# Linear attention y: the three transposes of the diagonal term ahead of the half-array matmuls

## The chip, the cores and the metric

One core of one Trainium2 chip runs the whole program. The metric is the device time of one execution in microseconds (us), taken as the median of several executions. The profile comes from one execution more, with the hardware profiler on.

## The reference, cut to what matters

Three layers follow each other: a linear attention with decay (4 batches, 8 heads, 768 steps, head size 48), a mixture of experts with causal softmax attention, and a channel mix. The change touches the first layer alone:

```python
for t in range(S):
    cur = u * k[t] (outer) v[t]              # the diagonal term
    y[t] = r[t] @ (state + cur)
    state = w[t][:, None] * state + k[t] (outer) v[t]
```

The kernel cuts the 768 steps into 6 chunks of 128. Within a chunk, y is the sum of three terms: the diagonal term (a number per step and head times v), the products of the chunk's earlier steps (`at`, a masked 128x128 matrix, times v), and, from the second chunk on, the state that came in (`um`) times r.

## The kernel before, in words

**Stages.** Stage A is the linear attention, one pair of heads at a time, 16 pairs in all. Stage B is the mixture of experts, one batch at a time. Stage C is the channel mix. Batch 0 of A runs by itself with the loading of B's weights; then the rest of A (`sA`) is woven with B (`sB`) and with the conversion of C's weights to two parts (`conv`). Once A is through, `c_weights` (L819 to L826) loads C's weights with DMAs from GpSimd, and the rest of B is woven with C.

**What sets the order.** `run_all` (L88) takes the next piece from the stream that is least far by written costs; `weave` (L75) puts the preparation of the next pair (`a_prep`) between the pieces of the present one (`a_pair`). That gives the order in which the program is written down. The framework then places each instruction on its engine's queue by its own estimate of when it can start, so an engine's queue holds nearly, but not exactly, the written order; an instruction that is ready early can come ahead of one that waits. Each engine then works its queue off in order.

**A pair of heads.** `a_prep` (L209) transposes w, k and r on TensorE (`ptr`, L201), runs two scans on VectorE (L220 `suf`, L246 `ex`) and makes the diagonal term `dg` on GpSimd (L261). `a_pair` (L318) calls `g_unit` three times (matmuls `pg` L329, copy on ScalarE L337, mask on GpSimd L338, result `at`), `a_u` once (matmuls `pu` L298, then `um` on VectorE L307 and L313) and `y_unit` twice, three chunks each; `a_kt` (transposes `pkt`, L286) belongs to the next pair.

**y_unit (L343 to L374).** One PSUM tile `py` holds three chunks of 128 columns side by side, head 0 in partitions 0 to 47 and head 1 in partitions 64 to 111. For each chunk in turn the diagonal term is transposed into its columns over the whole width of the array (L348, `dg` and the identity, 128x128); then matmuls add to it, each on one half of the array's columns (48 columns used, head 0 on the left half, head 1 on the right, L359): one of v and `at` per head, and, but for chunk 0, one of `um` and `rt` per head. The profile shows each of these fp32 matmuls as two instructions, so a chunk has one transpose and eight half-array instructions (four for chunk 0). Then ScalarE (L373) and VectorE (L374) split `py` into two parts `xs`, which go to HBM or into B's tile.

Other users of one half of the array's columns are `pu` (L298) and `pa` in B (L701). All other matmuls and transposes use its whole width.

Of the kernel before, what the change touches and what calls it, by code (L numbers as in the profile page):

```python
# [23 lines left out]
C = 128  # L24
# [88 lines left out]
def rwkv_moe_kernel(ctx, tc, r, k, v, w, u, wg, wq, wk, wv, wo, mu_k, mu_r, w_k, w_v, w_r, out):  # L113
    nc = tc.nc
# [20 lines left out]
    def ps_a(nm):  # L135
        tag = cyc["tags"][cyc["n"] % len(cyc["tags"])]
        cyc["n"] += 1
        return (psA if tag == "a" else ps).tile([128, 512], F32, tag=tag, name=nm, bufs=PSB[tag])
# [12 lines left out]
    ident = const.tile([128, 128], F32, name="ident")  # L151
# [126 lines left out]
    def a_kt(b, pr):  # L278
        kt = kts.pop((b, pr))
        n1 = NC_ - 1  # L280
        kh = pA.tile([128, n1 * 128], F32, tag="kh", name="kh", bufs=1)
        for c0, c1 in ((0, 3), (3, n1)):
            q = ps_a("pkt")
            m = (c1 - c0) * 128
            for c in range(c0, c1):
                nc.tensor.transpose(q[:, (c - c0) * 128 : (c - c0 + 1) * 128], kt[:, c * C : (c + 1) * C], ident)  # L286
            nc.scalar.copy(kh[:, c0 * 128 : c0 * 128 + m], q[:, 0:m])
        heads[b, pr] = kh

    def a_u(b, pr):  # L290
        rt, kt, vn, pc = prep[b, pr]
        kh = heads.pop((b, pr))
        n1 = NC_ - 1
        pu = ps_a("pu")
        for c in range(n1):
            for h in range(2):
                p0 = 64 * h
                nc.tensor.matmul(  # L298
                    pu[p0 : p0 + 64, c * D : (c + 1) * D],
                    lhsT=kh[:, c * 128 + p0 : c * 128 + p0 + 64],  # L300
                    rhs=vn[:, h * NC_ + c, 0:D],
                    start=True,
                    stop=True,
                )
        um = pA.tile([128, D * n1], F32, tag="um", name="um", bufs=2)
        uv = um.rearrange("p (d c) -> p d c", c=n1)
        nc.vector.tensor_tensor(  # L307
            out=uv,
            in0=pu[:, 0 : n1 * D].rearrange("p (c d) -> p d c", d=D),
            in1=pc[:, None, 1:NC_].to_broadcast([128, D, n1]),  # L310
            op=OP.mult,
        )
        nc.vector.tensor_tensor_scan(  # L313
            out=um, data0=pcxs[(b * NP + pr) % 2].rearrange("p d c -> p (d c)"), data1=um, initial=0.0, op0=OP.mult, op1=OP.add
        )
        return um

    def a_pair(b, pr, nxt):  # L318
        rt, kt, vn, pc = prep[b, pr]
        gs = []  # L320
        dg = dgs.pop((b, pr))
        xs = pA.tile([128, 2, S], F32R, tag="xs", name="xs", bufs=XSB)

        def g_unit(i):
            at = pA.tile([128, 2, 2, C], F32, tag="at", name="at", bufs=ATB)
            pg = ps_a("pg")
            for x in range(2):
                c = 2 * i + x
                nc.tensor.matmul(  # L329
                    pg[:, x * 2 * C : (x + 1) * 2 * C],  # L330
                    lhsT=kt[:, c * C : (c + 1) * C],
                    rhs=rt[:, c].rearrange("p h x -> p (h x)"),
                    start=True,
                    stop=True,
                )
            av = at.rearrange("p c h t -> p (c h t)")
            nc.scalar.copy(av, pg)  # L337
            nc.gpsimd.affine_select(  # L338
                out=av, in_=av, pattern=[[0, 4], [1, C]], compare_op=OP.is_gt, fill=0.0, base=0, channel_multiplier=-1
            )  # L340
            gs.append(at)

        def y_unit(i, um):  # L343
            py = ps_a("py")
            for x in range(3):
                c = 3 * i + x
                cols = slice(x * C, (x + 1) * C)
                nc.tensor.transpose(py[:, cols], dg[:, c].rearrange("p h x -> p (h x)"), ident)  # L348
                terms = []
                for h in range(2):  # L350
                    q = [(vn[:, h * NC_ + c], gs[c // 2][:, c % 2, h])]
                    if c > 0:
                        q.append((um[:, c - 1 :: NC_ - 1], rt[:, c, h]))
                    terms.append(q)
                n = len(terms[0])
                for j in range(n):
                    for h in range(2):
                        lt, rh = terms[h][j]
                        nc.tensor.matmul(  # L359
                            py[64 * h : 64 * h + D, cols],  # L360
                            lhsT=lt,
                            rhs=rh,
                            start=False,
                            stop=j == n - 1,
                            skip_group_check=True,
                        )
            sl = slice(i * HALF, (i + 1) * HALF)
            src, lo = py[:, 0:HALF], nc.vector
            if b * NP + pr in X_POOL:
                lo = nc.gpsimd  # L370
                src = xs[:, 1, sl].bitcast(F32)
                nc.scalar.copy(src, py[:, 0:HALF])
            nc.scalar.copy(xs[:, 0, sl], src)  # L373
            lo.tensor_tensor(out=xs[:, 1, sl], in0=src, in1=xs[:, 0, sl].bitcast(F32), op=OP.subtract)  # L374

        g_unit(0)
        yield 4 * 218
        um = a_u(b, pr)
        yield 10 * 110
        g_unit(1)  # L380
        yield 4 * 218
        g_unit(2)
        yield 4 * 218
        y_unit(0, um)
        yield 16 * 128
        if nxt is not None:
            a_kt(*nxt)
        yield 5 * 109
        y_unit(1, um)
        yield 18 * 128  # L390
        prep.pop((b, pr))
        for h in range(2):
            if b:
                f0 = (2 * pr + h) * D
                nc.sync.dma_start(
                    xd[b, :, f0 : f0 + D].rearrange("x p s -> p x s"), xs[64 * h : 64 * h + D].bitcast(F32)
                )
            else:
                o = 0
                while o < D:  # L400
                    kt_, p0 = divmod((2 * pr + h) * D + o, 128)
                    m = min(D - o, 128 - p0)
                    nc.sync.dma_start(
                        xts[0][p0 : p0 + m, :, kt_].bitcast(F32), xs[64 * h + o : 64 * h + o + m].bitcast(F32)
                    )
                    o += m
# [809 lines left out]
```

## Time and profile before

| | |
|---|---|
| median of 3 runs | 754.82 us (754.77 to 755.72) |
| the profiled execution: its own time | 753.42 us |
| the profiled execution: its span | 751.6 us |
| TensorE matmul busy | 692.0 us (92%) |
| VectorE busy | 502.2 us (67%) |
| ScalarE busy | 406.7 us (54%) |
| GpSimd busy | 293.5 us (39%) |
| TensorE's share of the chain that ended last | 66% |
| VectorE's share of that chain | 18% |

PE is TensorE's matmul, PEld its weight load, DVE VectorE, ACT ScalarE, POOL GpSimd, SP SyncE. The span is the time from the first to the last recorded instruction; the execution's own time is 1.8 us longer. The chain that ended last is followed back from the last instruction: at each step to what released it, or to the instruction ahead of it on its engine. Busy time of TensorE has modelled ends, so the distance from one start to the next is the better measure of what one of its instructions takes.

### The profile page before, as it was taken

Reading aid. Unit: us, or ns where it says so; the run is one execution under the profiler, and the core shown is the slowest. Engines: PE = TensorE matmul, PEld = TensorE weight load, DVE = VectorE, ACT = ScalarE, POOL = GpSimd, SP = SyncE. Lnnn points to the kernel's source line nnn. Section 1 sums busy time; section 2 is a strip of 40 time slices with the busy share of each in tenths; the row PEclk is TensorE's granted clock in tenths of the full one; section 3 lists DMA queues with packets and bytes.
Section 4 is the critical chain, followed back from the end, with each engine's and each line's share of the span. In section 5 each row is a group of like instructions: output and inputs, shape, how many; then the busy total and the mean of one; then the engine's idle time right before and its main releaser. Section 6 shows DMA issues by size and latency. Waiting matters only on the chain.

```text
span 751.6 us, 13686 instructions
## 1 busy us (share of the span) xinstructions
PE 692.0 (92%) x4938; PEld 590.2 (79%) x4938; DVE 502.2 (67%) x938; ACT 406.7 (54%) x1117; POOL 293.5 (39%) x397
## 2 busy tenths in 40 slices
PE   6998977989799999973999999999999999999996
PEld 4676755666577686752898998988999888999995
DVE  8989898898899759642474456756636674729620
ACT  3554564666566446642756466466554657453530
POOL 5966444233344222220635345344242525252320
PEclk8999988999899999995999999999999999999999
DMA  7788666669567552179021201060211020111001
GB/s 154 161 166 192 182 162 169 152 173 274 141 175 191 121 126 66 32 250 347 22 74 22 75 12 32 11 179 12 69 48 44 1 64 1 53 64 53 12 22 37
DMA packets 144205, 77.88 MB, mean 104 GB/s; under 512 B 109824, under 2 KB 138752, under 8 KB 143616
## 3 DMA queue, kind: packets, MB, share of 16 engines
q1 hardware_dynamic: 139936, 64.73, 33.9%
q0 software_dynamic: 864, 7.47, 2.5%
q10 hardware_dynamic: 3328, 4.72, 1.9%
q8 instruction: 41, 0.67, 0.4%
q14 instruction: 36, 0.29, 0.1%
HBM read 47.40 MB, written 23.99 MB: 95 GB/s over the span
## 4 chain that ended last, share of the span: by engine, by line
PE 66%; DVE 18%; DMA 6%; issue 3%; POOL 2%; ACT 2%; SPq 1%; DVEq 0%; POOLq 0%; ACTq 0%
PE ph L862 14%; PE pvo L862 13%; PE pa L701 6%; PE pz L862 5%; PE pq L509 4%; PE pt L672 4%; DVE suf L220 3%; PE py L359 3%; DMA k<-k 3%; PE po L509 3%; PE psc L615 3%; PE pv L509 2%; PE pg L329 2%; PE psc L616 2%; DVE ex L246 2%
## 5 line engine op out<-in xcount | busy, mean ns | idle before, releaser
L624 DVE TENSOR_REDUCE st<-psc 128x1 f32<-128x384 f32 (+4 forms) x128 | 62.5, 500 | 69.1 <-PE psc L620 61.0
L882 POOL TENSOR_TENSOR rl<-rl 128x256 f32<-128x256 f32 (+1 forms) x88 | 61.5, 702 | 100.1 <-ACT rl L881 96.6
L856 POOL TENSOR_TENSOR ml<-m,mh 128x256 fp32r<-128x256 f32 x54 | 40.6, 751 | 114.6 <-ACT mh L855 114.5
L636 ACT ACTIVATE A<-psc,st 128x384 f32<-128x384 f32 (+4 forms) x128 | 68.9, 543 | 27.1 <-DVE st L633 16.4
L862 PE MATMUL ph<-mh,ckh 128*128 128x256 f32 (+1 forms) x264 | 79.6, 302 | 2.1 <-DMA ckh<-ck_h_scratch 2.1
L862 PE MATMUL ph<-mh,ckl 128*128 128x256 f32 (+1 forms) x264 | 77.3, 293 | 0.0
L862 PE MATMUL ph<-ml,ckh 128*128 128x256 f32 (+1 forms) x264 | 77.2, 294 | 0.0
L338 POOL TENSOR_SCALAR_AFFINE_SELECT at<-at 128x512 f32<-128x512 f32 x48 | 41.7, 873 | 79.7 <-ACT at L337 79.3
L615 PE MATMUL psc<-k,q 128*128 128x384 f32 (+4 forms) x128 | 49.9, 390 | 20.9 <-DMA k<-k 15.7
L862 PE MATMUL pvo<-cvh,hh 128*128 128x384 f32 x192 | 65.1, 339 | 0.0
L862 PE MATMUL pvo<-cvl,hh 128*128 128x384 f32 x192 | 64.7, 337 | 0.0
L862 PE MATMUL pvo<-cvh,hl 128*128 128x384 f32 x192 | 64.3, 337 | 0.0
L885 POOL TENSOR_TENSOR hl<-rl,hh 128x256 fp32r<-128x256 f32 x72 | 53.3, 747 | 25.7 <-ACT hh L883 25.5
L329 PE MATMUL pg<-rt,kt 128*128 128x256 f32 x192 | 54.5, 412 | 7.8 <-DVE rt L255 3.4
L672 PE MATMUL pt<-ident,A 128*128 128x128 f32 x336 | 58.2, 278 | 1.2 <-ACT A L636 1.2
L852 DVE SCALAR_TENSOR_TENSOR m<-x2c,mu,m 128x256 f32<-128x256 f32 (+1 forms) x66 | 34.7, 530 | 36.4 <-ACT m L849 36.0
L862 PEld LDWEIGHTS ph<-mh,ckh 128*128 128x128 f32 x264 | 50.2, 190 | 4.9 <-ACT m L849 2.3
L881 ACT ACTIVATE rl<-ph 128x256 f32<-128x256 f32 (+1 forms) x88 | 35.5, 405 | 34.2 <-PE ph L862 27.3
L701 PE MATMUL pa<-at,vs 128*64 128x384 f32 (+2 forms) x288 | 52.9, 427 | 0.1
L855 ACT CAST mh<-m 128x256 fp32r<-128x256 f32 (+1 forms) x66 | 28.2, 427 | 43.7 <-DVE m L852 36.8
L862 PEld LDWEIGHTS ph<-ml,ckh 128*128 128x128 f32 x264 | 50.1, 190 | 0.3 <-issue 0.2
L862 PEld LDWEIGHTS ph<-mh,ckl 128*128 128x128 f32 x264 | 50.2, 190 | 0.0
(172 smaller groups left out, 1949.2 us busy)
## 6 DMA issues: line engine op xcount, KB each, us to landing
x_scratch<-xs SPq DMA_DIRECT2D x24, 288.0 KB, 3.8
x<-x_scratch SPq DMA_DIRECT2D x6, 1152.0 KB, 9.2
nw<-in_w_dram SPq DMA_DIRECT2D x32, 144.0 KB, 3.3
nk<-in_k_dram SPq DMA_DIRECT2D x32, 144.0 KB, 2.9
nr<-in_r_dram SPq DMA_DIRECT2D x32, 144.0 KB, 3.1
nv<-in_v_dram SPq DMA_DIRECT2D x16, 288.0 KB, 3.5
out_dram<-rg SPq DMA_DIRECT2D x24, 192.0 KB, 1.9
c_raw<-in_moe_w_k_dram SPq DMA_DIRECT2D x12, 256.0 KB, 3.6
```

The lines of the kernel that those rows point to most:

```text
L329: nc.tensor.matmul(pg[:, x * 2 * C : (x + 1) * 2 * C], lhsT=kt[:, c * C : (c + 1) * C], rhs=rt[:, c].rearrange("p h x -> p (h x)"), start= ...
L338: nc.gpsimd.affine_select(out=av, in_=av, pattern=[[0, 4], [1, C]], compare_op=OP.is_gt, fill=0.0, base=0, channel_multiplier=-1)
L509: nc.tensor.matmul(out, lhsT=a, rhs=c, start=i == 0, stop=i == n - 1)
L615: nc.tensor.matmul(o, lhsT=qs[e][:, tsl], rhs=ks[e][:, s0:s1], start=True, stop=False, skip_group_check=True)
L624: nc.vector.tensor_reduce(out=st[:, si : si + 1], in_=o, axis=AX.X, op=OP.max, negate=True)
L636: nc.scalar.activation(out=A[:, s0:s1], in_=p[:, 0 : s1 - s0], func=AF.Exp, bias=nm, accum_out=st[:, 3 + si : 4 + si])
L672: nc.tensor.transpose(pt[:, (j - j0) * 128 : (j - j0 + 1) * 128], A[:, j * 128 : (j + 1) * 128], ident)
L701: nc.tensor.matmul(pa[64 * e : 64 * e + 64, t0:HALF], lhsT=vs[:, j, 2 * pr + e], rhs=at[e][:, c0 : c0 + HALF - t0], start=j == 0, stop=j = ...
L856: eng.tensor_tensor(out=lo[:, j], in0=m1, in1=hi[:, j].bitcast(F32), op=OP.subtract)
L862: nc.tensor.matmul(out, lhsT=a, rhs=c, start=i == 0, stop=i == n - 1)
L882: nc.gpsimd.tensor_tensor(out=rl_, in0=rl_, in1=rl_, op=OP.mult)
L885: eng.tensor_tensor(out=hl[:, m], in0=rl_, in1=hh[:, m].bitcast(F32), op=OP.subtract)
```

## The change

The three transposes of a `y_unit` are issued first, then the half-array matmuls of its three chunks. The operands, the number of instructions and their shapes stay. The transposes are written out as matmuls with `is_transpose`; only the first of the three now carries the start flag for the bank.

```diff
         def y_unit(i, um):
             py = ps_a("py")
             for x in range(3):
+                nc.tensor.matmul(
+                    py[:, x * C : (x + 1) * C],
+                    lhsT=dg[:, 3 * i + x].rearrange("p h x -> p (h x)"),
+                    rhs=ident,
+                    start=x == 0,
+                    stop=False,
+                    is_transpose=True,
+                    skip_group_check=True,
+                )
+            for x in range(3):
                 c = 3 * i + x
                 cols = slice(x * C, (x + 1) * C)
-                nc.tensor.transpose(py[:, cols], dg[:, c].rearrange("p h x -> p (h x)"), ident)
                 terms = []
```

## Rows read from the trace of the kernel before

**Rows 1.** Busy time by stretch; columns: stretch, length, engines, PEclk, DMA share, GB/s

```profile
20.00:80.00 60.00, 55.96 (x495) 41.92 (x494) 54.60 (x81) 31.81 (x79) 42.66 (x42) 0.97 0.78 167
80.00:160.00 80.00, 66.33 (x507) 50.49 (x505) 70.61 (x149) 47.64 (x135) 29.09 (x34) 0.91 0.63 164
160.00:240.00 80.00, 71.05 (x552) 54.37 (x551) 71.52 (x143) 49.03 (x141) 33.03 (x41) 0.96 0.78 209
240.00:321.00 81.00, 78.70 (x679) 60.92 (x678) 60.12 (x121) 45.49 (x122) 19.65 (x23) 1.00 0.35 81
...
352.00:752.00 400.00, 392.22 (x2565) 361.39 (x2564) 220.71 (x411) 216.76 (x605) 152.10 (x220) 0.99 0.15 46
```

**Rows 2.** The chain that ended last, from 240 to 325 us, by line

```profile
by line: PE py L359 15.3%; PE pg L329 11.2%; DVE suf L220 7.0%; PE pv L509 6.8%; PE pq L509 6.4%; PE py L348 6.4%; PE pa L701 5.7%; DVE rt L255 4.6%; PE ptr L201 3.9%; PE pt L672 3.0%; PE po L509 2.8%; DVE q L146 2.0%; DVE ex L246 2.0%; DVE
```

**Rows 3.** TensorE's timeline, 287 to 293 us: start, length, what, count, idle before

```profile
289.07 0.33 PE L348 MATMUL py<-ident,dg 128*128 128x128 f32 x1
289.33 0.43 PE L359 MATMUL py<-at,nv 128*48 128x128 f32 x4
...
289.91 0.33 PE L348 MATMUL py<-ident,dg 128*128 128x128 f32 x1
...
290.74 0.33 PE L348 MATMUL py<-ident,dg 128*128 128x128 f32 x1
...
291.57 1.13 PE L329 MATMUL pg<-rt,kt 128*128 128x256 f32 x4
```

**Rows 4.** TensorE's timeline, 20 to 60 us: transposes in a row, chunks in a row

```profile
23.93 0.60 PE L286 MATMUL pkt<-ident,kt 128*128 128x128 f32 x4
24.37 0.27 PE L348 MATMUL py<-ident,dg 128*128 128x128 f32 x1
...
25.14 0.33 PE L348 MATMUL py<-ident,dg 128*128 128x128 f32 x1
25.31 0.38 PE L201 MATMUL ptr<-ident,nw 128*128 128x128 f32 x2
25.62 0.43 PE L359 MATMUL py<-at,nv 128*48 128x128 f32 x4
...
47.94 0.39 PE L359 MATMUL py<-rt,um 128*48 128x128 f32 x4
48.15 0.39 PE L359 MATMUL py<-at,nv 128*48 128x128 f32 x4
48.37 0.39 PE L359 MATMUL py<-rt,um 128*48 128x128 f32 x4
```

**Rows 5.** Timeline of TensorE's weight loads, 23.2 to 24.7 us

```profile
24.26 0.14 PEld L348 LDWEIGHTS py<-ident,dg 128*128 128x128 f32 x1
24.57 0.17 PEld L359 LDWEIGHTS py<-at,nv 128*48 128x48 f32 x4 [0.17 <-issue]
```

**Rows 6.** TensorE's timeline, 20 to 322 us: transposes alone between half-array matmuls, first and last

```profile
20.73 0.33 PE L348 MATMUL py<-ident,dg 128*128 128x128 f32 x1
...
319.94 0.33 PE L348 MATMUL py<-ident,dg 128*128 128x128 f32 x1
```

**Rows 7.** The chain in order of time: such transposes on it, first and last

```profile
40.69 0.26 PE py L348
...
320.01 0.26 PE py L348
```

**Rows 8.** TensorE's timeline, 316 to 321 us: other work behind a transpose

```profile
316.74 0.27 PE L348 MATMUL py<-ident,dg 128*128 128x128 f32 x1
316.77 0.42 PE L509 MATMUL pq<-x,wqh 128*128 128x384 f32 x1
```

**Rows 9.** Behind stage A: GpSimd's issue of C's weights (timeline), and a wait (chain)

```profile
327.07 0.73 POOL L824 DMA_DIRECT2D ckh<-ck_h_scratch  x1 [11.02 <-PE pt L672]
```

```profile
327.69 22.52 DMA k<-k
```

**Rows 10.** Busy time by stretches of 5 us, columns as in rows 1: the clock falls

```profile
195.00:200.00 5.00, 2.14 (x18) 1.31 (x17) 4.90 (x10) 2.32 (x7) 3.05 (x5) 0.94 0.61 149
200.00:205.00 5.00, 5.00 (x29) 3.15 (x30) 3.32 (x10) 2.63 (x9) 0.33 (x1) 0.50 0.06 17
```

## The prediction

> **What bounds the kernel now.** I read the busy times by stretch first. Up to 20 us the core fills its pipeline. From 20 to 240 us VectorE and TensorE are about equally full: 54.6 against 56.0 of 60 us, 70.6 against 66.3 of 80, 71.5 against 71.1 of 80. From 240 to 321 us TensorE leads, 78.7 of 81 us against VectorE's 60.1, and from 352 us on it has the kernel to itself, 392.2 of 400 [rows 1]. The change touches nothing behind about 321 us, where the last y is made.
>
> Next the chain of waits. From 240 to 325 us, where TensorE leads, the half-array matmuls of y are its largest item, 15.3%, and y's transposes have another 6.4% [rows 2]: 21.7% of 85 us, some 18 us. The reader is to see that in this stretch y is work on which the end waits; before 240 us much of it lies beside VectorE's scans.
>
> Last, TensorE's timeline of one undisturbed unit. The transposes start at 289.07, 289.91 and 290.74, and the work behind the unit at 291.57 [rows 3]: 2.50 us for three chunks, 0.833 each.
>
> **What a switch costs.** Transposes in a row come every 0.11 us: four take from 23.93 to 24.37 [rows 4]. A lone one between half-array matmuls holds the array 0.26 us, from 289.07 to 289.33 [rows 3]. Three between two runs of half-array matmuls, a transpose of y and two of `ptr`, take 0.48, from 25.14 to 25.62 [rows 4]; so each further one costs 0.11 and the rest is paid once a run. Half-array matmuls in a row come four per 0.21 to 0.22 us, from 47.94 over 48.15 to 48.37 [rows 4], thus eight per 0.44; a chunk with a switch at both ends takes 0.833 less 0.26, which is 0.57.
>
> **The unit after.** Three transposes 0.48, the first chunk with the way in and out 0.57, two more chunks of 0.44: 1.93 us in place of 2.50. Two round trips between full array and halves go, at 0.57 / 2 = 0.287 us each. The same two switches go in a unit with chunk 0, which has four matmuls fewer.
>
> What shows at a switch in the trace: within a run of transposes a weight load starts 0.11 us ahead of its matmul (24.26 against 24.37), while the first load of the halves starts only at 24.57, with the load queue idle for 0.17 us and nothing named that it waits for [rows 4, 5]. The Trainium skill ("TensorE: Matmul & The Clock Gate", Part 3, The mechanism) says that TensorE pulls weight loads ahead of matmuls in flight when they go to the background weight buffer. By that rule alone the switches are hidden and the sum is nothing; the row has the load late, and I go by the row.
>
> **How many switches go.** The diff takes two a unit from 32 units, 64 at most. The timeline shows fewer to be had, since the queue's order already mixes other work in: the transpose at 316.74, say, is followed by a projection of B, and costs no switch of its own [rows 8]. I count 51 transposes of y that stand alone between half-array matmuls, the first at 20.73, the last at 319.94 [rows 6]. All 51 would give 51 x 0.287 = 14.6 us of TensorE's time.
>
> **How much of it lies on the path.** The chain in order of time has 23 lone transposes with y's matmuls on both sides, from 40.69 to 320.01 [rows 7]: 13 behind 240 us, 10 ahead of it. That is 23 x 0.287 = 6.6 us if nothing takes over. Behind 240 us VectorE has room [rows 1], and I take the 13 in full, 3.7 us. Ahead of it VectorE is as full as TensorE, and its scans become the later of the two when TensorE shortens; I take half of 2.9 us, 1.4. The bounds for this half are 0 and 2.9 us; the whole has bounds 0 and 14.6, and I stay by the chain's count since it is nearest to what the end waits for.
>
> **What else moves.** Transposes two and three need `dg` and a free `py`, as the first one did, so they add no wait; they run ahead of the matmuls that wait for the mask (`at`) and for `um`. Those waits end when they did, with less left to do behind them. `py` is held no longer. No DMA is added or moved. ScalarE's and VectorE's reading of `py` starts with the unit's last matmul, as before. The start flag on one transpose alone changes no duration that a row shows; I cost it at nothing.
>
> **Behind stage A.** GpSimd issues the loads of C's weights at 327.07, after the last of A, and B's copies of k land behind them, a wait of 22.52 us on the chain [rows 9]. This hangs on A's end, so a shorter A pulls all of it forward and loses nothing. TensorE's 392.2 us after that are unchanged [rows 1].
>
> **Sum.** 3.7 + 1.4 = 5.1 us. The profiled execution took 753.4 us by itself, so 748.3 in its terms; it lies 1.4 us below the median of the runs shown, 754.8, from which I forecast **749.7 us**. A measurement of this kernel can tell about 0.2%, 1.5 us, from no change.
>
> **Rivals.**
> 1. *The time stays.* Either the switches stay, because the framework places other full-array work between the chunks' matmuls in place of the transposes, or VectorE takes over everywhere and the gain waits at its next scan. For it: 13 of the 64 switches are not there to save, and VectorE is above 88% busy to 240 us [rows 1]. Against it: behind 240 us VectorE has 21 us free [rows 1]. It gives 753.3 to 756.3. The skill's rule on loads pulled ahead, above, comes out here too, as 754.8; with the load late by 0.17 us [rows 5] I give it 0.02 of this chance.
> 2. *Slower, by the clock.* TensorE is granted half speed (0.50, which is 1.2 of 2.4 GHz) from 200 to 205 us, after it was busy for only 2.14 us of the 5 before [rows 10]. A TensorE that is done sooner with y waits longer for VectorE between 80 and 240 us, and could fall to 1.2 GHz more often. One such stretch costs at most half of its 5 us of busy time, 2.5 us. It decides from three new stretches on the path: 754.8 - 5.1 + 7.5 = 757.2. Against it: only 0.29 us is taken at each place, and the stretch behind 240 us, where most is gained, has a clock of 1.00 [rows 1]. The Trainium skill (same page, Part 4) says that transposes do not count as busy for the clock as matmuls do, so that runs of them would favour this; here transposes in a row kept 0.11 us each [rows 4], which is full speed by the trace.
> 3. *More than the sum.* The off-chain switches also count, because the waits that hid them move up with the rest; from 6.6 us for the chain in full towards 14.6: 748.2 down to 740.2. Against it is VectorE's fill ahead of 240 us.
>
> **How the numbers follow.** The forecast, 3 to 6.6 us gained, 0.50. A smaller gain, 1.5 to 3 us, by a VectorE that takes over more, 0.13. Rival 3, 0.08. Rival 1, 0.17. Rival 2, and any other loss by a new order of the queues, 0.12. So faster 0.71, same 0.17, slower 0.12. The range, from 746.0 (a little of rival 3) to 755.6 (the middle of rival 1), leaves out most of rival 2 and the tail of rival 3, together a little under 0.2.
>
> **What would show it.** In the timeline after, y's transposes stand three in a row, 0.11 us apart, with some 0.2 us to the first half-array matmul, and a clean unit of three full chunks takes 1.93 us. Lone transposes of y fall from 51 to a few. Stage A's last y ends about 5 us sooner, GpSimd's issue of C's weights moves by the same, and the stretch from there to the end keeps its length. I am wrong in the step of the path if y units take 1.9 us and the end of A has not moved; in the step of the price if they still take 2.5; and by rival 2 if PEclk from 80 to 240 us is lower than 0.91 and 0.96.

## The result, and the profile after

The changed kernel takes **727.2 us** against 754.8 before: ratio 0.965, interval [0.9612, 0.9688]. It is faster by 27.6 us where 5.1 were forecast, and lies 18.8 us below the foot of the range. The profiled execution took 727.1 us, with a span of 725.4.

**The unit.** TensorE's timeline of the changed kernel, from 299 to 302 us; columns as in [rows 3]:

```profile
299.35 0.49 PE L346 MATMUL py<-ident,dg 128*128 128x128 f32 x3
299.77 0.42 PE L368 MATMUL py<-at,nv 128*48 128x128 f32 x4
300.02 0.39 PE L368 MATMUL py<-rt,um 128*48 128x128 f32 x4
300.24 0.39 PE L368 MATMUL py<-at,nv 128*48 128x128 f32 x4
300.46 0.39 PE L368 MATMUL py<-rt,um 128*48 128x128 f32 x4
300.68 0.39 PE L368 MATMUL py<-at,nv 128*48 128x128 f32 x4
300.89 0.39 PE L368 MATMUL py<-rt,um 128*48 128x128 f32 x4
301.21 0.44 PE L518 MATMUL pq<-x,wqh 128*128 128x384 f32 x1
```

The reader is to see three transposes in one row of the view, 0.42 us to the first half-array matmul, and then half-array matmuls without a break. The unit takes 1.86 us from its first start to the work behind it, against 2.50 in [rows 3]. Of the 51 lone transposes of y, none is left.

**The stages.** Busy time by stretch in the changed kernel, columns as in [rows 1], with stage A as a whole and what lies behind it:

```profile
20.00:80.00 60.00, 51.79 (x466) 40.95 (x462) 52.75 (x76) 30.77 (x76) 46.17 (x42) 0.91 0.77 169
80.00:160.00 80.00, 68.54 (x582) 56.71 (x579) 75.56 (x160) 52.37 (x146) 32.29 (x37) 0.98 0.67 174
160.00:240.00 80.00, 70.45 (x567) 53.77 (x565) 73.58 (x143) 49.30 (x139) 35.11 (x38) 0.98 0.74 193
...
0.00:313.90 313.90, 274.02 (x2323) 221.25 (x2323) 275.08 (x516) 184.96 (x495) 144.13 (x168) 0.97 0.66 159
313.90:725.40 411.50, 398.76 (x2616) 364.16 (x2616) 222.82 (x423) 224.23 (x622) 155.60 (x229) 1.00 0.20 68
```

The cuts are where ScalarE begins to read the last `py`. The same two rows of the kernel before:

```profile
0.00:320.90 320.90, 284.55 (x2291) 217.72 (x2292) 273.08 (x510) 181.55 (x490) 136.48 (x168) 0.95 0.64 155
320.90:751.60 430.70, 407.42 (x2648) 372.43 (x2648) 229.09 (x429) 225.14 (x628) 157.04 (x229) 0.97 0.20 66
```

Stage A is 7.0 us shorter, near the 5.1 forecast (how far that is luck stands under the prediction's errors). The stretch behind it, of which I had said that it keeps its length, is 19.2 us shorter. TensorE also has 32 instructions fewer to do there (2616 against 2648) and 32 more ahead of the cut. Each row is one execution, and three kernels with one TensorE order up to the cut reach it at 317.5, 320.9 and 324.7 us (last section), so a few us in the length of a stage say little by themselves; 19.2 us are more than that.

**The end of stage A.** Where the 19.2 us went is seen in the timeline. The kernel before, what SyncE, GpSimd and TensorE issue there:

```profile
324.78 0.47 SPq L562 DMA_DIRECT2D k<-k  x1
...
327.04 0.60 SPq L520 DMA_DIRECT2D x<-x_scratch  x1
327.07 0.73 POOL L824 DMA_DIRECT2D ckh<-ck_h_scratch  x1 [11.02 <-PE pt L672]
...
327.69 1.24 SPq L562 DMA_DIRECT2D k<-k  x2
...
328.98 0.60 SPq L520 DMA_DIRECT2D x<-x_scratch  x1
...
329.62 11.28 SPq L562 DMA_DIRECT2D k<-k  x1
...
350.35 0.66 PE L615 MATMUL psc<-k,q 128*128 128x384 f32 x1 [12.63 <-DMA k<-k]
```

Three of B's four copies of k (SyncE, L562) are issued behind the first load of C's weights. The scores (`psc`) need them, and TensorE stands idle 12.6 us for them. They also stand behind SyncE's own loads of B's next input x (L520, 1152 KB each). Those land at 348.10 and 356.91 us, 21.1 and 27.9 us after their issue, and each of the three copies lands 0.2 to 4.2 us behind the x load ahead of it. The changed kernel:

```profile
308.16 1.55 SPq L571 DMA_DIRECT2D k<-k  x2
...
312.92 0.97 SPq L529 DMA_DIRECT2D x<-x_scratch  x2
...
313.98 1.44 SPq L571 DMA_DIRECT2D k<-k  x2
...
325.50 0.73 POOL L833 DMA_DIRECT2D ckh<-ck_h_scratch  x1 [14.92 <-PE pt L681]
```

All four copies are issued 10 us or more ahead of C's loads. Two of them still stand behind the x loads, but these now take 5.5 and 9.5 us; the two copies land 9.1 and 8.4 us after their issue, and TensorE waits 0.5 us for k. The reason stands in TensorE's queue: 144 of the projection matmuls (`pq`) are placed ahead of the last y, in place of 117, so k is there earlier. The diff does not touch them; the framework came to another order. What TensorE does in the former wait, first before, then after:

```profile
327.70:350.30 22.60, 6.75 (x40) 3.98 (x39) 3.66 (x8) 5.09 (x15) 4.32 (x9) 0.68 1.09 384
350.30:370.00 19.70, 19.54 (x126) 16.31 (x127) 11.13 (x23) 13.87 (x45) 9.55 (x15) 0.84 0.33 115
```

```profile
327.70:350.30 22.60, 18.86 (x129) 16.05 (x128) 11.29 (x25) 16.58 (x49) 9.63 (x17) 1.00 0.92 360
```

Busy 6.75 us against 18.86; and the clock, at 1.2 GHz for a part of the wait and for some us behind it (0.68 and 0.84 of full speed), stays at 2.4 GHz (1.00).

### The profile page after: what moved, and what is told of

Same layout as the page of the kernel before. It is cut to its first block, busy times and chain, and to the rows that moved or that the text cites. A ratio compares the mean times of both kernels' runs of the same rounds, so it can differ in the third digit from the quotient of the medians.

```text
span 725.4 us, 13681 instructions
## 1 busy us (share of the span) xinstructions
PE 672.8 (93%) x4938; PEld 585.4 (81%) x4938; DVE 497.9 (69%) x938; ACT 409.2 (56%) x1117; POOL 299.7 (41%) x397
## 4 chain that ended last, share of the span: by engine, by line
PE 64%; DVE 18%; DMA 8%; issue 4%; ACT 3%; POOL 1%; SPq 1%; ACTq 0%; DVEq 0%; POOLq 0%
PE ph L871 14%; PE pvo L871 14%; PE pz L871 5%; PE pa L710 5%; PE pq L518 4%; PE pt L681 3%; PE po L518 3%; PE py L368 3%; PE pv L518 3%; DMA c_raw<-in_moe_w_v_dram 2%; DVE ex L246 2%; PE psc L624 2%; PE pg L329 2%; DVE suf L220 2%; DVE rt L255 2%
## 5 line engine op out<-in xcount | busy, mean ns | idle before, releaser
L891 POOL TENSOR_TENSOR rl<-rl 128x256 f32<-128x256 f32 (+1 forms) x88 | 59.3, 678 | 78.5 <-ACT rl L890 78.3
L338 POOL TENSOR_SCALAR_AFFINE_SELECT at<-at 128x512 f32<-128x512 f32 x48 | 44.7, 932 | 79.2 <-ACT at L337 79.0
L329 PEld LDWEIGHTS pg<-rt,kt 128*128 128x128 f32 x192 | 34.4, 197 | 19.8 <-DVE um L307 6.8
```

Source lines behind the costliest of these rows:

```text
L329: nc.tensor.matmul(pg[:, x * 2 * C : (x + 1) * 2 * C], lhsT=kt[:, c * C : (c + 1) * C], rhs=rt[:, c].rearrange("p h x -> p (h x)"), start= ...
L338: nc.gpsimd.affine_select(out=av, in_=av, pattern=[[0, 4], [1, C]], compare_op=OP.is_gt, fill=0.0, base=0, channel_multiplier=-1)
L891: nc.gpsimd.tensor_tensor(out=rl_, in0=rl_, in1=rl_, op=OP.mult)
```

## The experiments

Two theories stood against each other: the gain has two parts (fewer switches, and another order at the end of A), or all of it is the switches' doing. A third says that all of it is the order. The lone transposes and the projections ahead of the last y, which the expectations name, are counted in TensorE's queue of each kernel. The diffs below are against the kernel before where nothing else is said.

**One pair's transposes first.**

```diff
+            early = range(3) if b * NP + pr == 0 else ()
+            for x in early:
+                tr(x)
...
+                if x not in early:
+                    tr(x)
```

(`tr(x)` is the written-out transpose of the change.) 

> The transposes come first in the first pair of heads alone; the other 15 pairs are as before, so 53 lone transposes of y stay in TensorE's queue. By itself this little edit makes the framework place 144 of the projection matmuls (pq) ahead of the last y, as in the changed kernel, in place of 117. Theory one (two parts: switches cost about 12 us of stage A, and the order at the end of A, with k's copies ahead of C's weight loads, is worth about 14 us): 739 to 743 us, with the long wait for k gone. Theory two (all of the 27.6 us comes from the switches): 753 to 755, nothing beyond two units' switches. Theory three (all of it is the order): 727 to 730.

Measured: 734.9 us, ratio 0.9746 [0.9714, 0.9777]. Two units of 32 are changed and 19.8 us of 27.6 are there. Its last y is read at 322.1 us, so stage A is 1.2 us longer than before, and the rest takes 410.6 us in place of 430.7:

```profile
0.00:322.10 322.10, 289.62 (x2326) 222.90 (x2326) 276.06 (x517) 186.06 (x496) 144.81 (x168) 0.96 0.64 155
322.10:732.70 410.60, 399.39 (x2615) 365.39 (x2614) 224.84 (x422) 224.66 (x621) 153.35 (x229) 0.99 0.21 68
```

Theory two falls. The order alone is worth more than theory one had put on it (14), and less than theory three's whole.

**The last 8 pairs' transposes first**: the same with `range(3) if b * NP + pr >= 8 else ()`. 

> The transposes come first in the last 8 pairs of heads; 26 lone transposes stay, 25 are gone, and 116 projection matmuls stand ahead of the last y, as in the kernel before. Theory one: half of the switches' 12 us and none of the order's 14, so 747 to 750 us, with the wait for k of about 22 us still there. Theory two: half of 27.6, so 740 to 742. Theory three: 754 to 755.

Measured: 745.4 us, 0.9878 [0.9849, 0.9907], 2 us below what theory one gave. The old order stays, but the wait changed too: two of the four copies of k landed in 8.4 and 9.2 us, where before three took 22.5 and more, and the rest takes 426.0 us in place of 430.7. These two were issued ahead of SyncE's x loads, one of them 0.6 us behind the first of C's; the fourth copy, behind the x loads, took 27.4 us. Stage A is only 0.3 us shorter. So about half of this gain again lies behind A (the profiled execution took 748.5 us, 3.1 more than the median), and this run does not price the switches.

**Two more transposes a unit, in front or between.** Against the changed kernel; they write to columns 384 to 511 of `py`, which nobody reads, and add 64 transposes to the work:

```diff
+            for _ in range(2):
+                <transpose of dg[:, 3 * i] into py[:, HALF : HALF + C]>
             for x in range(3):
                 c = 3 * i + x
...
+                if x:
+                    <the same transpose>
```

The first addition is the one run, the second the other. 

> The changed kernel with two more transposes in each unit, written to columns of the bank that nobody reads, in one run with the other three: no switch more, 64 transposes more at 0.11 us. All theories: 727 plus at most 7 us of TensorE's time, 730 to 734. It is the partner of the next run, which has the same extra transposes at another place.

> The same 64 extra transposes, but one ahead of the second and one ahead of the third chunk's matmuls, so that the switches of the kernel before are back (54 lone transposes) while the order at the end of stage A is that of the changed kernel (143 projection matmuls ahead of the last y). Theory one: 54 switches at 0.287 us are 15.5 us of TensorE's time, of which some 12 reach the end: 742 to 746. Theory two (27.6 us for 49 switches, 0.56 each): about 760. Theory three: as the run before, 730 to 734.

Measured: 732.6 us, 0.9717 [0.9692, 0.9743], and 747.2 us, 0.9907 [0.9877, 0.9937]. The same instructions in the new order, with and without the switches, differ by 14.6 us: 0.27 us for each of 54, nearly the 0.287 that was read from the trace. In the profiled executions the last y is read at 321.6 and at 334.7 us, 13.1 us apart, or 0.24 for each; the rest differs by another 3.7 us, in which SyncE's copies of k and loads of x come in another order. So most of the price falls in stage A, and 0.24 to 0.27 us is what the pair shows. The timeline of the run with the transposes between shows the switches back, 0.83 us from one lone transpose to the next:

```profile
332.93 0.33 PE L359 MATMUL py<-ident,dg 128*128 128x128 f32 x1
333.19 0.43 PE L378 MATMUL py<-at,nv 128*48 128x128 f32 x4
333.44 0.39 PE L378 MATMUL py<-rt,um 128*48 128x128 f32 x4
333.76 0.33 PE L359 MATMUL py<-ident,dg 128*128 128x128 f32 x1
```

**The control: written as the change has it, in the order of before** (`early = ()`). 

> Control: the transposes are written out as in the changed kernel, with the start flag on the first of a unit alone, but each stands ahead of its own chunk's matmuls, as before; 51 lone transposes, 117 projection matmuls ahead of the last y. All theories: 754 to 756, as the kernel before; any gain here would belong to the flag.

Measured: 752.9 us, 0.9974 [0.9948, 1.0], a little under the 754 expected and not clear of no change. The flag and the written-out form are not the cause.

**C's weight loads behind k's copies**, in the kernel before:

```diff
-    def c_weights(pW):
+    def c_weights(pW, behind=()):
...
                 t = pW.tile([128, n0, n1], F32R, name=nm + x)
+                for e, kt_ in enumerate(behind):
+                    o = 64 - 64 * e
+                    nc.gpsimd.tensor_copy(t[o : o + 1, 0, 0:2], kt_[o : o + 1, HALF - 1 : HALF + 1])
...
-        c_weights(pW)
+        while (1, 1) not in qk:
+            sB[2] += next(sB[0])
+        c_weights(pW, qk[1, 1][1])
```

(The loop writes B's pieces up to these copies ahead of the loads.) 

> The kernel before, all switches kept and 117 projection matmuls ahead of the last y, with one thing changed: each of C's weight loads first waits, by a copy of two elements on GpSimd, until the four copies of k have landed. Theory one (of the 20 us that the order is worth, the most is k's copies waiting behind the weight loads, with the clock that falls meanwhile): the wait for k of 22.5 us falls below 5, the loads start some 5 us later, and the time is 737 to 743. Rival (what counts is that 27 projection matmuls are done before A's end, under its waits): 754 to 760, since the loads only start later.

Measured: 742.5 us, 0.9849 [0.9798, 0.99]. No y and no projection has moved, all switches are there, and 12.0 us are gone, though the loads start 10.3 us later (337.33 in place of 327.07). TensorE's wait for k in this run, from its waits:

```profile
PE psc L615 <- DMA k<-k: 3.5, 1, 3.5
```

3.5 us in place of 12.6. SyncE's x loads stand ahead of the copies as before, but land after 8.5 and 10.4 us in place of 21.1 and 27.9, and the three copies behind them after 8.1 to 8.4. The rest behind the last y takes 419.5 us, 11.2 less than before (in an execution 3.8 us under the median). So C's loads, running while k's copies are under way, are a cause, and not only a companion, of the lost time.

**The second copy of k by ScalarE**, in both kernels: `DUP = "act"` in place of `"dma"`. 

> The kernel before with all switches, where ScalarE writes the second copy of k (64x384, about 0.47 us each, 32 of them) in place of a DMA, so no transfer of k can stand behind the weight loads. The framework places 144 projection matmuls ahead of the last y here. Theory one: as the run with pair 0 alone, 733 to 738. If the 20 us hang on something else than k's transfer and the projections' place: 750 or more.

> The changed kernel with ScalarE writing the second copy of k. Its trace has two waits of 9 us for k's transfers near the end of A, with TensorE mostly busy beside them. Theory one: the order's gain is already taken, so 723 to 728. If k's transfers still cost the changed kernel much: below 722.

Measured: 739.1 us, 0.9779 [0.9725, 0.9832], and 737.8 us, 0.9771 [0.9724, 0.9818]. The first is 1 us outside its expectation; its rest takes 412.6 us, 18.1 less than before, so what was gained lies where it was expected, while stage A ends at 327.4, 6.5 us later than before. The second is a miss by 10 us: with ScalarE copying, the change gives only 1.3 us. Stage A ends at 323.1 us there, 9.2 later than in the changed kernel, at a mean clock of 0.95 against 0.97. Why A comes out longer in both was not settled.

**Two of three transposes first, and all but the last two pairs** (`early = range(2)`; `range(3) if b * NP + pr < 14 else ()`). 

> Two of a unit's three transposes come first, the third stays ahead of its chunk: 24 lone transposes in place of 51, and the order at the end of A is that of the changed kernel (144 projection matmuls ahead of the last y). Theory now: the order gives its 20 us in full, and the switches what they gave between the run with pair 0 alone (734.9, 53 lone) and the changed kernel (727.2, none), 0.15 us each: 730 to 732. If the switches' part were not a price per switch but an accident of one order: 727 or 735 are as likely.

> The transposes come first in the first 14 pairs of heads, as before in the last two, where TensorE has the stretch to itself: 8 lone transposes, 144 projection matmuls ahead of the last y. Theory now: 8 x 0.15 to 8 x 0.29 us above the changed kernel, 728 to 730. If the order at the end of A hung on the last pairs' own transposes: 745 or more.

Measured: 730.1 us, 0.9653 [0.9603, 0.9704], and 728.6 us, 0.965 [0.9602, 0.9698]. With the new order in all four, 53, 24, 8 and 0 lone transposes give 734.9, 730.1, 728.6 and 727.2 us: a fall of 7.7 us, 0.15 for each on the average. Only the first step is clear: as ratios to the kernel before, the last three are 0.9653, 0.965 and 0.965, closer than their intervals are wide, so an even price for each is not shown.

**The loads behind k's copies, in the changed kernel**: the diff of the run above on top of the change. 

> The changed kernel with the wait of the run in which C's weight loads stand behind k's copies. In the changed kernel k's copies are issued some 11 us ahead of the loads already, so if that wait's 12 us in the kernel before came from k's copies standing behind the loads, it has nothing to give here: 726 to 731. If holding the loads back is worth something by itself (less traffic while B goes on): 715 to 720.

Measured: 728.9 us, 0.9689 [0.9641, 0.9736]. The wait that gave 12.0 us in the kernel before gives nothing where k's copies are ahead of C's loads anyway. None of the kernels beats the changed one.

## Why the prediction was wrong

The step that failed is the one on what follows stage A: "This hangs on A's end, so a shorter A pulls all of it forward and loses nothing", and with it "No DMA is added or moved". No DMA is written elsewhere, but in the framework's placing 27 projection matmuls moved ahead of the last y, k's copies moved with them, and they passed C's weight loads. The stretch of which I said that it loses nothing became 19.2 us shorter. I had read the 22.52 us in [rows 9] as a fixed cost that is carried along; it was a cost of one queue order, and the change, as two units of it alone do, tipped that order over.

The measured sum, by runs that differ in one thing: 754.6 to 734.9 us by the order (two units' transposes first), and 734.9 to 727.2 by the other switches. Of the 20.1 us by which the rest is shorter in the first step, holding C's loads back gives 11.2 by itself in the kernel before. Another 4.6 is work moved, not saved: 26 more projection matmuls (counted to the cut, the 27 to the last y itself) at 0.177 us (nine took 1.59 us on the changed kernel's chain) are done ahead of the cut. The remaining 4.3 us were not told apart.

*The price of a switch* was right. (0.57 / 2 is 0.285, not 0.287, which changes no result.) The unit was forecast at 1.93 us and takes 1.86; the three transposes in [rows 4] stood behind half-array matmuls, while the unit shown here stands behind other transposes and is spared the way in. The pair with the extra transposes paid 0.24 to 0.27 us a switch.

*The share on the path* was right in kind and a little small: 5.1 us forecast, 7.7 measured between the run with one pair and the changed kernel. I took the chain's 23 switches and then half of those ahead of 240 us; the runs show them all together at half price, 0.15 of 0.287 on the average. That VectorE takes over part of it fits the pair with the extra transposes, where TensorE has more work, little is taken over, and the price is nearly whole; that it is VectorE was argued, and no run took VectorE's work away. How much a switch is worth differs from kernel to kernel: 0.24 to 0.27, 0.15, and almost nothing with ScalarE's copies (1.3 us for 53). Why was not settled. That stage A ended 7.0 us sooner, near the forecast, is partly luck: between the run with one pair and the changed kernel it became 8.2 us shorter, and the new order had made it 1.2 us longer, with 26 projection matmuls more to do in it.

*The rivals.* The time did not stay. The clock did not fall more often: from 80 to 240 us it is 0.98 and 0.98, against 0.91 and 0.96 in [rows 1], and only from 20 to 80 us it is lower, 0.91 against 0.97. The third rival, by off-chain switches, reached down to 740.2 us only, 13 above the time measured; all the switches together gave 7.7 us between the run with one pair and the changed kernel, and 14.6 where they cost most. Not among them was a gain by another order of the queues. I did write that "the framework places other full-array work" elsewhere, but only against the gain and inside a unit, and in the chances "a new order of the queues" stands as a loss alone. The range's upper end has a slip of its own: the middle of the first rival is 754.8, not 755.6.

The Trainium skill's rule on weight loads pulled ahead ("TensorE: Matmul & The Clock Gate", Part 3, The mechanism) would by itself have made the switches free. The fall from 2.50 to 1.86 us a unit and the 14.6 us between the two runs with extra transposes say that they are not, at this kind of switch.

## What to carry to other kernels

Where a framework places the instructions, a small move early in a program can change the order of queues far behind it; the first thing to compare after such a change is which DMAs stand ahead of which at the stage borders, on the same queue and beside it. A long wait on the chain for a small transfer behind bulk loads was no fixed cost here: ask what put it there, give both orders a price, and let them widen the range. If the order is worth something, hold it by a dependency, as the run with the loads behind k's copies does, and do not leave it to chance.

## What was not expected of the hardware

A copy of 96 KB of k lands 2.0 to 2.1 us after its issue with nothing large under way, 8.1 to 9.1 us behind SyncE's x loads alone (changed kernel and loads held back), 8.4 and 9.2 beside C's weight loads but ahead of the x loads (last 8 pairs), and 22.5 to 27.5 behind the x loads and beside 7 MB of C's loads (before). By these rows the long wait needs both; no run took the x loads away. Transfers of the two issuing engines did pass each other: in the kernel before, a load of C's issued at 329.35 us landed at 350.07, ahead of the copy of k issued at 327.69, which landed at 350.21. And the mean clock over stage A differed among kernels whose TensorE order is the same up to the last y: 0.95, 0.94 and 0.96 in the kernel before, the control and the run with the loads behind k's copies, with the last y read at 320.9, 324.7 and 317.5 us. The later the end, the lower the clock; which of the two brings the other was not settled. Single executions differ by these few us without any edit to TensorE's order, which is why the switches' 7.7 us are taken from medians.
